# A spectral mixer and MLP on one core: batch 0's gathers on GpSimd's queue, the second stage two groups ahead, and a reordered opening

## The chip, the cores and the metric

The kernel runs on one core of one Trainium2 chip. The core has five engines, each with an instruction queue of its own that it works through in order: TensorE (PE; its weight loads are listed as PEld), VectorE (DVE), ScalarE (ACT), GpSimd (POOL) and SyncE (SP), which only issues transfers. Transfers (DMA) are issued from the queues of SP, ACT and POOL. The metric is the time of one execution on the device in microseconds (us). Each kernel is run several times, and the median is compared.

## The reference

The inputs are x of 8 x 3072 x 256, four parameters of a complex linear layer of width 256, and two weights of an MLP of width 2048; all is fp32.

```python
X = np.fft.rfft(x, axis=1)
Yr = Xr @ w_r - Xi @ w_i + b_r
Yi = Xr @ w_i + Xi @ w_r + b_i
Y = soft(Yr, 0.01) + 1j * soft(Yi, 0.01)     # sign(v) * max(|v| - 0.01, 0)
y = np.fft.irfft(Y, n=3072, axis=1)
h = y.reshape(8 * 3072, 256) @ w_in
out = (max(h, 0) + log1p(exp(-abs(h)))) @ w_out
```

## The kernel before, in words

The Fourier transform of 3072 = 96 x 32 points is split into small matrix products. For each batch:

- **s1** (first stage) is a product of length 96 over 512 columns of x; batch 0 has 16 of them, and their results stay on the chip in `a0`. For batch 1 ten such products are made ahead of the main loop, and the rest by `s1_four`, which does four matmuls of half width in one piece of the main loop; their results go to memory (`a_dr`).
- **s3** (second stage): `NP` = 12 groups. `load_a` gathers a group's operand `ap` from `a0` (for batch 0) in two halves, each from 4 rows to 128 rows of the chip's memory, into one of three buffers; four matmuls follow.
- **mix** (`mix_direct`): the complex layer. Its operand is split into a high part (ScalarE, rounded to fp32r) and a low part (VectorE, `less`, L119), and each product is three matmuls (`mm3`, L249 to L251), 24 a group. ScalarE also makes a negated copy (`minus`). Group 0 needs two corrected copies, called `real`. VectorE then adds the bias and does the soft threshold in three steps (L462 to L467; `z`, `cl`).
- **s4** (third stage): one matmul a group. Its result `d` goes partly to memory (`d_dr`) and, for batch 0, partly by two small gathers (`near`, L522) into `first_d`.
- **s5** (final stage): products over all groups give a block of tokens. For the first two blocks `first_tokens` turns four such products into the sums and differences B11, B21, T1 to T4 and B22, each split into a high and a low part.

The MLP is done with seven block products in place of eight, for two token blocks and two blocks of `w_in` at once (`ffn1`, banks `psc` and `pse`), a softplus, and `ffn2` into `pso`. The main loop has four slots for each step of it; `slot_products` and `slot_second` write them out. All spectral work of later batches, the splitting of the weights (`split_w`, eight of `w_in` and eight of `w_out`) and their stores are laid between the slots.

Everything stands in an order written out by hand. `first` lists the products ahead of the main loop and gives them negative indices up to -1; the main loop starts at index 0. `at(i, f)` puts anything else at an index, `turns` has for each weight the index of its split, that of its load and the staging buffer, and `later` holds work until the next index. At each index the program writes slot products, weight steps, the product, what `at` put there, and what was put off, and each engine gets its instructions in that order. A transfer that waits for its data holds up what stands behind it on its queue. Ahead of the main loop 6 banks of PSUM are used in turn (`psf`).

## Time and profile before

| | |
|---|---|
| median of 3 runs | 2607.09 us (2602.97 to 2609.22) |
| profiled execution, its own time | 2604.86 us |
| its span, first to last instruction | 2603.0 us |
| mean granted TensorE clock | 0.998 |
| PE busy | 2571.5 us (99% of the span) |
| ACT, DVE busy | 1672.2 us (64%), 1669.4 us (64%) |
| POOL busy | 166.8 us (6%) |

Busy times are sums over the whole span, and the opening (some 108 us ahead of the main loop) is a small part of it; stages have to be looked at one by one. A busy PE is not PE at its peak, since the ends of matmuls are modelled.

### The profile page before, as it was taken

The page shows a single profiled execution, that of the slowest core. Times are in us where ns is not written, and L with a number is a line of the kernel's source. Part 1 is how long each engine was busy: PE and PEld are TensorE (multiplying, and loading weights), DVE is VectorE, ACT ScalarE, POOL GpSimd, SP SyncE. Part 2 cuts the span into 40 slices and gives each one's busy share as a digit, 9 for nine tenths or more (in the row PEclk, how much of TensorE's full clock was granted, in tenths as well). Part 3 has the DMA queues.
Part 4 walks back from the last instruction along what each step waited for, and adds up shares of the span by engine and source line. Part 5 has one row for each costly group of instructions (what it writes and reads, how often), then busy time and mean ns, then how long its engine had stood idle before and what let it go on. Part 6 is the DMA issues. An engine that isn't in the chain of part 4 may idle for free.

```text
span 2603.0 us, 36237 instructions
## 1 busy us (share of the span) xinstructions
PE 2571.5 (99%) x13161; PEld 2128.4 (82%) x13161; DVE 1669.4 (64%) x2812; ACT 1672.2 (64%) x3025; POOL 166.8 (6%) x198
## 2 busy tenths in 40 slices
PE   7999999999999999999999999999999999999999
PEld 5677888888788888888888888888888888888887
DVE  4888775677566775666746767466674666645454
ACT  4676666666666666666666666666666666666665
POOL 2320000000000000000000000000000000000000
PEclk9999999999999999999999999999999999999999
DMA  8875555655646555565555665556645545445543
GB/s 248 255 237 189 176 185 167 214 185 160 206 159 195 169 181 190 166 193 186 163 191 178 187 194 163 184 174 182 210 159 169 180 158 188 140 159 183 175 150 113
DMA packets 187085, 472.53 MB, mean 182 GB/s; under 512 B 22252, under 2 KB 88844, under 8 KB 186908
## 3 DMA queue, kind: packets, MB, share of 16 engines
q1 hardware_dynamic: 182636, 466.01, 56.3%
q0 software_dynamic: 2912, 2.58, 0.4%
q8 instruction: 104, 1.70, 0.3%
q10 hardware_dynamic: 1360, 1.64, 0.2%
q14 instruction: 73, 0.60, 0.1%
HBM read 383.09 MB, written 82.71 MB: 179 GB/s over the span
## 4 chain that ended last, share of the span: by engine, by line
PE 94%; DVE 3%; DMA 1%; ACT 1%; issue 1%; POOL 0%; SPq 0%; DVEq 0%; POOLq 0%; ACTq 0%
PE pso L249 14%; PE pso L251 13%; PE pso L250 13%; PE psc L249 7%; PE psc L251 7%; PE psc L250 7%; PE pse L249 5%; PE pse L250 5%; PE pse L251 5%; PE psf L560 5%; PE psf L251 3%; PE psf L250 3%; PE psf L249 3%; PE psf L365 3%; PE psf L330 2%; PE psf L292 1%
## 5 line engine op out<-in xcount | busy, mean ns | idle before, releaser
L697 DVE TENSOR_TENSOR gl<-t,gh 128x512 fp32r<-128x512 f32 x768 | 532.1, 693 | 328.1 <-ACT gh L691 325.8
L676 ACT COPY t<-psc 128x512 f32<-128x512 f32 x576 | 337.8, 586 | 524.2 <-PE psc L251 522.0
L681 DVE TENSOR_TENSOR t<-pse,t 128x512 f32<-128x512 f32 x576 | 396.1, 688 | 401.0 <-ACT t L676 275.7
L249 PE MATMUL pso<-gh,w 128*128 128x512 f32 x1536 | 621.6, 405 | 0.0
L251 PE MATMUL pso<-gh,w 128*128 128x512 f32 x1536 | 600.1, 391 | 0.0
L250 PE MATMUL pso<-gl,w 128*128 128x512 f32 x1536 | 599.9, 391 | 0.0
L691 ACT CAST gh<-t 128x512 fp32r<-128x512 f32 x768 | 477.1, 621 | 60.9 <-PE pso L251 37.5
L687 ACT ACTIVATE t<-t 128x512 f32<-128x512 f32 x576 | 365.1, 634 | 65.9 <-DVE t L681 64.8
L249 PEld LDWEIGHTS pso<-gh,w 128*128 128x128 f32 x1536 | 289.8, 189 | 91.3 <-issue 41.9
L251 PEld LDWEIGHTS pso<-gh,w 128*128 128x128 f32 x1536 | 288.8, 188 | 62.6
L250 PEld LDWEIGHTS pso<-gl,w 128*128 128x128 f32 x1536 | 290.0, 189 | 49.3
L249 PE MATMUL psc<-y_sb,w 128*128 128x512 f32 x768 | 300.7, 392 | 3.0 <-ACT t L676 2.7
L251 PE MATMUL psc<-y_sb,w 128*128 128x512 f32 x768 | 299.8, 390 | 0.0
L250 PE MATMUL psc<-y_sb,w 128*128 128x512 f32 x768 | 298.8, 389 | 0.0
L599 POOL TENSOR_TENSOR y_sb<-raw,y_sb 128x512 fp32r<-128x512 f32 x69 | 104.7, 1518 | 2148.1 <-ACT y_sb L596 2148.1
L249 PE MATMUL pse<-y_sb,w 128*128 128x512 f32 x576 | 226.1, 393 | 3.1 <-DVE t L681 3.0
L250 PE MATMUL pse<-y_sb,w 128*128 128x512 f32 x576 | 224.4, 390 | 0.0
L251 PE MATMUL pse<-y_sb,w 128*128 128x512 f32 x576 | 224.4, 390 | 0.0
L249 PEld LDWEIGHTS psc<-y_sb,w 128*128 128x128 f32 x768 | 144.2, 188 | 36.0 <-ACT t L676 4.8
L251 PEld LDWEIGHTS psc<-y_sb,w 128*128 128x128 f32 x768 | 144.2, 188 | 31.2
L250 PEld LDWEIGHTS psc<-y_sb,w 128*128 128x128 f32 x768 | 144.2, 188 | 29.9
L498 DVE TENSOR_TENSOR shrunk<-z,cl 64x256 f32<-64x256 f32 x336 | 141.1, 420 | 6.2
(163 smaller groups left out, 3344.9 us busy)
## 6 DMA issues: line engine op xcount, KB each, us to landing
w<-w_dr SPq DMA_DIRECT2D x190, 896.0 KB
w<-w_dr SPq DMA_DIRECT2D x185, 512.0 KB
out_y<-ot SPq DMA_DIRECT2D x96, 256.0 KB
dp<-d_dr SPq DMA_DIRECT2D x57, 384.0 KB
ap<-a_dr SPq DMA_DIRECT2D x168, 128.0 KB
d_dr<-d SPq DMA_DIRECT2D x84, 256.0 KB
x<-in_x SPq DMA_DIRECT2D x104, 192.0 KB
a_dr<-a SPq DMA_DIRECT2D x102, 192.0 KB
```

Of the source, the lines that this page charges most:

```text
L249: nc.tensor.matmul(ps, wh, xh, start=start, stop=False, skip_group_check=more)
L250: nc.tensor.matmul(ps, wh, xl, start=False, stop=False, skip_group_check=more)
L251: nc.tensor.matmul(ps, wl, xh, start=False, stop=stop, skip_group_check=more)
L365: nc.tensor.matmul(xv[:, g, k], t[:, g, k * P:(k + 1) * P], g1_t[:, g].rearrange("p (c s) -> p c s", c=2), start=True, stop=True,)
L498: v.tensor_tensor(out=t[dst], in0=z[src], in1=cl[src], op=ALU.subtract)
L560: nc.tensor.matmul(ps[:, t - blk * BLK:t - blk * BLK + n], d_sb[b, blk // 2, n2 // 4][0][:, n2 % 4, k * P:(k + 1) * P], d_sb[b, blk // 2, ...
L599: eng.tensor_tensor(out=lo, in0=raw[j], in1=hi.bitcast(F32), op=ALU.subtract)
L676: nc.scalar.copy(t, banks[bank])
L681: nc.vector.tensor_tensor(out=t, in0=banks[bank], in1=t, op=ALU.add)
L687: nc.scalar.activation(t, banks[bank] if bank else t, AF.Softplus)
L691: nc.scalar.copy(gh, ct[key, what])
L697: nc.vector.tensor_tensor(out=gl, in0=ct.pop((key, what)), in1=gh.bitcast(F32), op=ALU.subtract)
```

## The change

It rewrites the order ahead of the main loop:

- Two matmuls on a tile of ones come first on PE.
- Gathers of batch 0 (`load_a`): four halves stay on SP's queue (the first of groups 0 to 3), twenty go to GpSimd's. Before, fifteen were on SP's and nine on GpSimd's. They may be asked for as soon as s3 of three groups before is done.
- s3 runs two groups ahead of the mix; every third group's operand has a buffer of its own (`l`), which the staging of two weights leaves.
- The constants `g1` come in five pieces rather than three, and most of them, the bias and the first weight behind the first gathers; the two mixing matrices come earlier and are split earlier.
- The copies `real` move from GpSimd to VectorE.
- The last group's second small gather is issued by SP (before: ACT).
- Twelve s1 products of batch 1 rather than ten stand ahead of the main loop, two of them between the last two s4; one `s1_four` less is in the main loop. Their stores are held until just ahead of the main loop.
- s5 is done in another order, and `first_tokens` is rewritten for it; one `snap` in the first step of the main loop stands earlier.

```diff
-        (1, 1, -48, -63, 'dp', 0),
+        (1, 1, -46, -51, 'dp', 0),
         (0, 0, -43, -49, 'raw', 1),
-        (1, 2, -38, -44, 'l', 0),
+        (1, 2, -38, -44, 'x1', 0),
...
-        (0, 2, -23, -29, 'l', 0),
+        (0, 2, -23, -29, 'x1', 0),
         (1, 4, -18, -24, 'dp', 0),
-        (1, 0, -13, -19, 'w64', 1),
+        (1, 0, -14, -19, 'w64', 1),
...
+        elif b and c >= 10:
+            xt = fours[1][:, (c - 10) * 512:(c - 9) * 512]
...
-        store(a_dr[b][:, 2 * c:2 * c + 2, :], a[16:].rearrange("p (n c) -> p n c", n=2), ("a", b))
+        dst, src = a_dr[b][:, 2 * c:2 * c + 2, :], a[16:].rearrange("p (n c) -> p n c", n=2)
+        if c < 4:
+            store(dst, src, ("a", b))
+        else:
+            held.append((dst, src, ("a", b)))
...
-                (nc.gpsimd if g and gp > 2 else nc.sync).dma_start(t[:, g, :], a0[16 + 2 * gp + g:16 + N1:NG])
+                (nc.gpsimd if g or gp > 3 else nc.sync).dma_start(t[:, g, :], a0[16 + 2 * gp + g:16 + N1:NG])
...
-            l = w1_tile()
+            l = sb.tile([P, 2 * 768], F32R, tag="l", name="l", bufs=1) if gp % 3 == 2 else w1_tile()
...
-                    nc.gpsimd.tensor_copy(r, t[:, 0:2, :P])
+                    nc.vector.tensor_copy(r, t[:, 0:2, :P])
                     for o in (0, 64):
-                        nc.gpsimd.memset(r[:, :, o:o + 1].bitcast(F32), 0.0)
+                        nc.vector.memset(r[:, :, o:o + 1].bitcast(F32), 0.0)
...
-                    (nc.scalar if gp >= 10 else nc.gpsimd).dma_start(first_d[2 * gp + g::NG].rearrange("q n c -> q (n c)"), dg[:4 * 12, g])
+                    (nc.gpsimd if gp < 10 else nc.sync if g and gp == NP - 1 else nc.scalar).dma_start(first_d[2 * gp + g::NG].rearrange("q n c -> q (n c)"), dg[:4 * 12, g])
...
         if what == 0:
             y_sb[key] = sb.tile([P, 16 * BLK], F32R, tag="y0", name="y_sb", bufs=1)
-            whole(key, B11, ps)
-            keep(key, 0, ps)
-        elif what == 1:
-            whole(key, B21, ps)
-            first_ps.append(ps)
+            both = sb.tile([P, 2 * BLK], F32, tag="raw", name="raw", bufs=1)
+            raw[0], raw[1] = both[:, :BLK], both[:, BLK:]
+            raw[2] = sb.tile([P, BLK], F32, tag="t", name="t", bufs=5)
+            a(tokens(key, B11)[0], ps)
+            a(raw[0], ps)
+            low(B11, raw[0])
         elif what == 2:
-            keep(key, 1, ps)
+            a(raw[1], ps)
             v(out=raw[0], in0=ps, in1=raw[0], op=ALU.subtract)
-        else:
-            raw[2] = sb.tile([P, BLK], F32, tag="t", name="t", bufs=5)
+            a(tokens(key, T1)[0], raw[0])
+        elif what == 3:
+            held_ps.append(ps)
             v(out=raw[2], in0=ps, in1=raw[0], op=ALU.subtract)
             v(out=raw[1], in0=ps, in1=raw[1], op=ALU.subtract)
-            split_token(key, T2, 2, nc.vector)
-            split_token(key, T3, 1, nc.vector)
+            a(tokens(key, T2)[0], raw[2])
+            a(tokens(key, B22)[0], ps)
+            low(T2, raw[2])
+        else:
+            a(tokens(key, B21)[0], ps)
+            a(tokens(key, T3)[0], raw[1])
+            low(B21, ps)
+            low(T3, raw[1])
+
+            low(T1, raw[0])
...
+        ones = sb.tile([P, 512], F32, tag="t", name="ones", bufs=5)
+        nc.vector.memset(ones, 1.0)
+        for _ in range(2):
+            nc.tensor.matmul(psf(), ones[:, :P], ones, start=True, stop=True)
         nc.gpsimd.dma_start(g3_sb, g3)
...
-        for i in range(NP + 3):
-            if i < NP:
-                first.append(("s3", 0, i))
-            if i >= 3:
-                first.append(("s4", 0, i - 3))
-            if 1 <= i <= NP:
-                first.append(("mix", 0, i - 1))
-
-        first += [("s1", 1, c) for c in range(4, 10)]
-        first += [("s5", j, k) for j, k in ((0, 0), (0, 1), (1, 0), (1, 1))]
+        first += [("s3", 0, 0), ("s3", 0, 1)]
+        for i in range(NP):
+            if i + 2 < NP:
+                first.append(("s3", 0, i + 2))
+            if i >= 2:
+                first.append(("s4", 0, i - 2))
+            first.append(("mix", 0, i))
+        first += [("s4", 0, NP - 2), ("s1", 1, 4), ("s1", 1, 5), ("s4", 0, NP - 1)]
+        first += [("s1", 1, c) for c in range(6, 12)]
+        first += [("s5", j, k) for j, k in ((0, 0), (1, 0), (1, 1), (0, 1))]
...
-                at(max(t - 7, t0 + 16), load_a, b, i)
+                at(max(t - 7, t0 + 16, first.index(("s3", 0, max(i - 3, 0))) + t0 if i > 2 else t0), load_a, b, i)
...
-        for t, i, j in ((t0 + 1, 0, 4), (t0 + 4, 4, 12), (t0 + 18, 12, NG)):
+        for t, i, j in ((t0 + 2, 0, 4), (t0 + 16, 4, 8), (t0 + 18, 8, 12), (t0 + 26, 12, 18), (t0 + 32, 18, NG)):
             at(t, nc.sync.dma_start, g1_0[:, i:j], g1[:, NG + i:NG + j])
-        at(t0 + 5, nc.sync.dma_start, bias0, bias_0)
+        at(t0 + 17, nc.sync.dma_start, bias0, bias_0)
...
-            at(t0 + 2, load_mix, k)
-            at(t0 + 17 + k, split_mix, k)
+            at(t0, load_mix, k)
+            at(t0 + 13 + k, split_mix, k)
...
+        for i in range(4):
+            at(i - 4, release, 2)
...
-        plan_s1(1, 4, 4, 5)
+        plan_s1(1, 4, 4, 6)
```

What the change moves on three queues, at the places that the text below speaks of. First GpSimd's queue at the start, before (`a_78` is `a0`; L219 to L221 are GpSimd's steps of a weight, L402 and L404 the copies `real`):

```order
L774 DMA x_96<-in_g 128x256
L349 DMA ap<-a_78 128x1x256
L219 ISA
L219 TENSOR_TENSOR y_79<-wt,wu 128x256
L220 TENSOR_TENSOR wt<-wt,wu 128x128
L221 TENSOR_TENSOR y_79<-wt,wu 128x128
L349 DMA ap<-a_78 128x1x256
L402 COPY real<-w_242 128x256
L404 MEMSET real 128x2 x2
```

The same queue after the change (L366 are the gathers, L223 a step of another weight, L539 the small gathers into `first_d`):

```order
L810 DMA x_96<-in_g 128x256
L366 DMA ap<-a_78 128x1x256 x8
L219 ISA
L219 TENSOR_TENSOR y_79<-wt,wu 128x256
L220 TENSOR_TENSOR wt<-wt,wu 128x128
L221 TENSOR_TENSOR y_79<-wt,wu 128x128
L366 DMA ap<-a_78 128x1x256 x2
L223 TENSOR_TENSOR w_225<-wt,wu 128x512
L539 DMA dp<-d 4x12x256 x2
L366 DMA ap<-a_78 128x1x256 x2
```

Eight gathers now stand in one row ahead of the first weight's steps, and later ones behind a weight's step. VectorE's queue from its first instruction on, before (the first weight, staged in `dpt`, has steps L197 to L203; L119 on `wml` splits a mixing matrix, on `w` it makes the mix operand's low part):

```order
L197 TENSOR_SCALAR wt<-dpt 128x512
L198 SCALAR_TENSOR_TENSOR wt<-dpt,wt 128x512
L119 TENSOR_TENSOR wml<-stage,wmh 128x2x256
L201 SCALAR_TENSOR_TENSOR wt<-wu,wt 128x512
L202 TENSOR_SCALAR wu<-wt 128x512
L203 TENSOR_TENSOR wu<-dpt,wu 128x512
L119 TENSOR_TENSOR wml<-stage,wmh 128x2x256
L119 TENSOR_TENSOR w_242<-psf,w_242 128x4x128
```

And after the change (L419 and L421 are the copies `real`):

```order
L807 MEMSET ones 128x512
L119 TENSOR_TENSOR wml<-stage,wmh 128x2x256 x2
L119 TENSOR_TENSOR w_233<-psf,w_233 128x4x128
L419 COPY real<-w_233 128x256
L421 MEMSET real 128x2 x2
L419 COPY real<-w_233 128x256
L421 MEMSET real 128x2 x2
L197 TENSOR_SCALAR wt<-dpt 128x512
L198 SCALAR_TENSOR_TENSOR wt<-dpt,wt 128x512
L119 TENSOR_TENSOR w_245<-psf,w_245 128x4x128
```

The first weight's five steps and the copies `real` now follow the first low part. SP's queue at the end of the third stage, as one piece of the difference (`w_dr` are stores of split weights, of which `w_dr_84` is the fifth of `w_in`; `dp<-d` is a small gather into `first_d`):

```order
 L237 DMA w_dr_90<-wp 128x1024
-L534 DMA dp<-in_hm 96x1152
+L283 DMA x_97<-in_x 96x512
 L237 DMA w_dr_84<-y_79 128x1792
-L104 DMA a_dr<-y_79 96x512
-L309 DMA x_97<-in_x 48x2x512 x2
+L539 DMA dp<-d 4x12x256
+L237 DMA w_dr_80<-w_978 128x1792
+L179 DMA y_79<-in_w_in 128x2x512
+L326 DMA x_96<-in_x 48x2x512 x2
 L104 DMA a_dr<-y_79 96x512 x2
```

The last group's second small gather now stands on SP behind the store of that weight.

## Rows read from the trace of the kernel before

**Rows 1.** The page: busy time of each engine, share of the span, instructions.

```profile
PE 2571.5 (99%) x13161; PEld 2128.4 (82%) x13161; DVE 1669.4 (64%) x2812; ACT 1672.2 (64%) x3025; POOL 166.8 (6%) x198
```

**Rows 2.** Busy time (and instructions) of each engine by stretch; granted clock, DMA share, GB/s.

```profile
26.00:97.00 71.00, 59.17 (x411) 50.84 (x411) 59.68 (x109) 34.37 (x71) 30.35 (x50) 0.99 0.79 239
...
300.00:2500.00 2200.00, 2199.66 (x11302) 1835.38 (x11301) 1399.72 (x2349) 1424.65 (x2577) 109.27 (x114) 1.00 0.56 177
```

**Rows 3.** PE in order of time: two mixes a group apart, final stage, main loop.

```profile
48.94 0.68 PE L249 MATMUL psf<-wmh,w 128*128 128x256 f32 x1
...
53.56 0.68 PE L249 MATMUL psf<-wmh,w 128*128 128x256 f32 x1
...
103.17 5.47 PE L560 MATMUL psf<-dp 96*128 96x96 f32 x48
...
108.45 0.48 PE L249 MATMUL psc<-y_sb,w 128*128 128x512 f32 x1
```

**Rows 4.** PE's waits from 26 to 97 us: total, times, longest.

```profile
PE psf L251 <- DVE w L119: 4.6, 4, 2.3
...
PE psf L365 <- DMA ap<-a: 3.2, 4, 1.6
...
PE psf L512 <- DVE z L467: 2.2, 1, 2.2
```

**Rows 5.** VectorE in order of time: first low part, last step of the last threshold.

```profile
28.77 0.69 DVE L119 TENSOR_TENSOR w<-psf,w 128x512 fp32r<-128x512 f32 x1 [0.87 <-ACT w L388]
...
94.55 0.69 DVE L467 TENSOR_TENSOR z<-z,cl 128x512 f32<-128x512 f32 x1
```

**Rows 6.** VectorE's busy time (and instructions) in two stretches; clock, DMA share, GB/s.

```profile
0.00:28.70 28.70, 4.13 (x7) 1.00 0.80 233
...
28.70:95.25 66.55, 56.21 (x103) 1.00 0.83 250
```

**Rows 7.** VectorE's waits from 28.7 to 95.3 us: total, times, longest.

```profile
DVE z L465 <- PE psf L251: 2.8, 1, 2.8
...
DVE w L119 <- ACT w L388: 2.1, 2, 1.2
...
DVE y L228 <- POOL y L221: 1.4, 1, 1.4
```

**Rows 8.** PE in order of time, first stage: start, length, engine, line, operation.

```profile
5.46 7.81 PE L292 MATMUL psf<-xt,x 96*128 96x512 f32 x12 [5.46 <-DMA xt<-in_x]
...
13.11 7.03 PE L292 MATMUL psf<-dp,x 96*128 96x512 f32 x16
...
19.98 1.88 PE L292 MATMUL psf<-x,x 96*128 96x512 f32 x4
```

**Rows 9.** The chain that ended last, by time: an early gather on SP.

```profile
23.30 3.77 DMA ap<-a
```

**Rows 10.** The line of the gathers (L349): GpSimd's issues, and until its gathers landed.

```profile
L349 POOL DMA_DIRECT2D ap<-a x9: 685/697/721, 28.5 to 73.3; - x9
...
DMA to landing us min/median/max: 6.1/7.5/8.9
```

**Rows 11.** Busy time by stretch as in group 2: three stretches with different DMA shares.

```profile
24.00:28.00 4.00, 2.68 (x12) 1.26 (x10) 3.01 (x5) 3.45 (x8) 0.00 (x0) 1.00 0.27 96
...
46.00:84.00 38.00, 36.05 (x264) 32.05 (x262) 34.35 (x63) 21.33 (x46) 20.36 (x30) 1.00 0.89 261
...
90.00:94.50 4.50, 3.16 (x22) 2.33 (x20) 4.36 (x10) 2.52 (x5) 2.86 (x6) 1.00 0.55 166
```

**Rows 12.** Small gathers by GpSimd's queue (L522): 46 to 84 us, then 89 to 94.

```profile
DMA to landing us min/median/max: 4.9/6.3/8.5
...
DMA to landing us min/median/max: 2.3/2.5/2.6
```

**Rows 13.** ScalarE's queue in order of time: the last group's small gathers.

```profile
97.81 1.63 ACTq L522 DMA_DIRECT2D dp<-d  x2
```

**Rows 14.** PE in order of time: four first-stage matmuls in the main loop.

```profile
121.46 1.09 PE L330 MATMUL psf<-x,f 48*64 48x512 f32 x8
```

More of the change, by code (lines that the diff above doesn't have):

```diff
@@ L172, in load_w @@
             st = sb.tile([P, 1024], F32, tag="raw", name="w64", bufs=1)
-        elif place == "l":
-            st = sb.tile([P, 2 * 768], F32R, tag="l", name="w64", bufs=1).bitcast(F32)[:, :1024]
+        elif place == "x1":
+            st = fours[1][:, :1024]
         elif place == "w64":
@@ L296, in s1, with release @@
             return
-        a = a1[:, c % 4] if c < 8 else g1_0[:16 + N1, 4 * (c - 8) + 16:4 * (c - 8) + 20].rearrange("p g n -> p (g n)")
-        nc.scalar.copy(a, ps[:16 + N1, :])
-        store(a_dr[b][:, 2 * c:2 * c + 2, :], a[16:].rearrange("p (n c) -> p n c", n=2), ("a", b))
+        if c < 8:
+            a = a1[:, c % 4]
+        elif c < 10:
+            a = g1_0[:16 + N1, 4 * (c - 8) + 16:4 * (c - 8) + 20].rearrange("p g n -> p (g n)")
+        else:
+            a = sb.tile([P, 512], F32, tag="a", name="a")[:16 + N1]
+        nc.scalar.copy(a, ps[:16 + N1, :])
+        dst, src = a_dr[b][:, 2 * c:2 * c + 2, :], a[16:].rearrange("p (n c) -> p n c", n=2)
[3 more added lines that the diff above has]
+            held.append((dst, src, ("a", b)))
+    held = deque()
+    def release(n):
+        for _ in range(n):
+            store(*held.popleft())
     def load_four(b, c):
@@ L604, in put_split, with low @@
         split_token(*args) if early else later.append(lambda: split_token(*args))
-    first_ps = []
+    held_ps = []
     def first_tokens(what, ps):
         key = 0, 0
-        v = nc.vector.tensor_tensor
+        v, a = nc.vector.tensor_tensor, nc.scalar.copy
+        def low(i, src):
+            hi, lo = tokens(key, i)
+            v(out=lo, in0=src, in1=hi.bitcast(F32), op=ALU.subtract)
         if what == 0:
             y_sb[key] = sb.tile([P, 16 * BLK], F32R, tag="y0", name="y_sb", bufs=1)
-            whole(key, B11, ps)
-            keep(key, 0, ps)
-        elif what == 1:
-            whole(key, B21, ps)
-            first_ps.append(ps)
+            both = sb.tile([P, 2 * BLK], F32, tag="raw", name="raw", bufs=1)
[4 more added lines that the diff above has]
+            low(B11, raw[0])
@@ L619, in first_tokens @@
         elif what == 2:
-            keep(key, 1, ps)
+            a(raw[1], ps)
             v(out=raw[0], in0=ps, in1=raw[0], op=ALU.subtract)
-        else:
-            raw[2] = sb.tile([P, BLK], F32, tag="t", name="t", bufs=5)
+            a(tokens(key, T1)[0], raw[0])
+        elif what == 3:
+            held_ps.append(ps)
             v(out=raw[2], in0=ps, in1=raw[0], op=ALU.subtract)
             v(out=raw[1], in0=ps, in1=raw[1], op=ALU.subtract)
-            split_token(key, T2, 2, nc.vector)
-            split_token(key, T3, 1, nc.vector)
-            def second():
-                split_token(key, T1, 0, nc.vector)
-                whole(key, B22, ps)
-                third()
-            def third():
-                v(out=raw[2], in0=first_ps[0], in1=raw[2], op=ALU.subtract)
-                later.append(lambda: split_token(key, T4, 2, nc.vector))
+            a(tokens(key, T2)[0], raw[2])
+            a(tokens(key, B22)[0], ps)
+            low(T2, raw[2])
+        else:
+            a(tokens(key, B21)[0], ps)
[3 more added lines that the diff above has]
+            low(T1, raw[0])
+            def second():
+                v(out=raw[2], in0=ps, in1=raw[2], op=ALU.subtract)
+                nc.gpsimd.tensor_copy(tokens(key, T4)[0], raw[2])
+                low(B22, held_ps[0])
+                later.append(lambda: low(T4, raw[2]))
@@ L740, in slot_products @@
             ffn1(key, "e", S3, T3)
+            if not prev:
+                snap(key, C21, "c")
             softplus(key, C11)
             high(key, C11)
-            snap(key, C21, "c")
+            if prev:
+                snap(key, C21, "c")
             low(key, C11)
@@ L792, in plan_s1 @@
                 at(t - 2 if b == 1 else t - 4, fold, b, c)
-                at(-8 if (b, c) == (1, 5) else t - 7, load_four, b, c)
+                at(t - 7, load_four, b, c)
         def plan_mix(b, start, step):
@@ L829, in tile_spectral_mixer_mlp @@
                 product(t, s1, b, i)
-                at(t0 + 23 + 3 * (i - 4) if b and i >= 4 else t0 - 1 + b, load_x, b, i)
+                at(i - 27 if b and i >= 10 else t0 + 23 + 3 * (i - 4) if b and i >= 4 else t0 - 1 + 2 * b, load_x, b, i)
             elif what == "s3":
                 product(t, s3, b, i)
-                at(max(t - 7, t0 + 16), load_a, b, i)
+                at(max(t - 7, t0 + 16, first.index(("s3", 0, max(i - 3, 0))) + t0 if i > 2 else t0), load_a, b, i)
             elif what == "mix":
@@ L856, in tile_spectral_mixer_mlp @@
         for i, (t, src) in enumerate(((g3h, g3_hi), (g3l, g3_lo))):
-            at(3 * i - 9, nc.gpsimd.dma_start, t, src)
-        at(-10, nc.gpsimd.memset, fours[1][32:64, :1024], 0.0)
-        at(-1, nc.gpsimd.memset, fours[0][32:64, :1024], 0.0)
+            at(3 * i + 8, nc.gpsimd.dma_start, t, src)
+        at(-3, nc.gpsimd.memset, fours[1][32:64, :1024], 0.0)
+        for i in range(4):
+            at(i - 4, release, 2)
+        at(-4, nc.gpsimd.memset, fours[0][32:64, :1024], 0.0)
         at(-1, early.clear)
```

## The prediction, made before the change was run

> **What bounds the kernel now.** I read the page's busy line first, then busy time by stretch, then PE's and VectorE's waits in the stretch that stands out, and last the rows at its two ends. The page says PE is busy 99% of the span [rows 1], and from 300 to 2500 us it is busy 2199.66 of 2200 us [rows 2]: there only fewer matmuls would help. The opening is different. From 26 to 97 us, twelve groups of batch 0 pass through the second stage (s3), the mix and the third stage (s4), and PE is busy 59.17 of 71 us [rows 2]. A group that waits for nothing takes 53.56 - 48.94 = 4.62 us [rows 3], twelve take 55.4 us, so about 15.6 us of the stage are waiting. PE's named waits there are VectorE's low parts of the mix operand (4.6 us), gathers (3.2) and the last soft threshold (2.2) [rows 4]; the rest is many short ones.
>
> VectorE is the other half of the stage. Its first low part starts at 28.77 and its last threshold ends at 94.55 + 0.69 = 95.24 [rows 5]. In these 66.5 us it works 56.2 and idles 10.3 [rows 6]: 2.8 until the first mix product, 2.1 for ScalarE's evacuations, 1.4 for GpSimd's part of the first weight [rows 7], and smaller pauses. PE needs 55.4 us and VectorE 56.2, yet the stage takes over 66, since each waits for the other. All that the change can reach is these 10 to 15 us, some 2.5 us at the start and a few around the start of the main loop.
>
> **The change part by part.** *Two matmuls on ones.* The first twelve matmul records (six products, two records each) take 5.46 to 13.11, 7.65 us; the next sixteen 13.11 to 19.98, 0.43 us each [rows 8]. At that pace twelve take 5.2 us, so 2.5 us are lost, as if about six records had run at half pace, TensorE's 1.2 GHz level, until some 5 us after its first matmul (read from the pace alone: the profile's clock holds no change before 10 us). The new matmuls are four records of that size, 3.4 us at half pace, in the time before the first x lands (5.46), when PE has nothing to do. If they start near 1.5 us (my estimate) and the pace again rises 5 us after the first, one or two slow records stay of six: 2.0 us saved, bounds 0 (the pause before 5.46 undoes it) and 2.5.
>
> *First gathers.* They may start 2.0 us earlier, near 20.5. On SP a gather landed 3.77 us after its issue [rows 9], and the last half of the first group came at 23.30 + 3.77 = 27.07. Now that half comes by GpSimd's queue, where gathers took 6.1 to 8.9 us [rows 10]. I take a value just over the lower end, 6.3, because little else moves then: DMA share 0.27 from 24 to 28 against 0.89 from 46 to 84 [rows 11]. So it lands near 26.8, and VectorE's first low part moves from 28.77 to 28.5 only. Bounds: 26 (GpSimd at the 2.5 us of small gathers at low DMA load [rows 12], so that SP's half, 20.5 + 3.8, decides) and 31 (8.9).
>
> *Second stage two groups ahead, and VectorE's order.* VectorE gets more to do between its first low part and its last threshold: the first weight's five steps, which stood ahead (seven instructions, 4.13 us before 28.7 [rows 6], less two splits of 0.69: 2.8), and the copies called real, taken over from GpSimd (0.7 for two of half width by the 0.69 of 512 columns [rows 5], 1.0 with four tiny fills). Six instructions now follow the last threshold, two of some 0.6 and four of a quarter width: -2.0. So 56.2 + 2.8 + 1.0 - 2.0 = 58.0 us. Of the idle 10.3 us, the three waits of [rows 7], 6.3 us, should go: with two more groups evacuated ahead there is always a low part or a weight step at hand. What stays is 4.0; new is about 1 at the start, where the second real copy needs ScalarE's negation, which stands behind the second group's evacuation; against that, fewer gathers and loads in front of the weights on SP's queue give back some 1.5. I take 3.5, bounds 2 and 8. The last threshold then ends at 28.5 + 58.0 + 3.5 = 90.0, **5.2 us earlier**. PE does not forbid it: twelve groups from about 31 end near 87.
>
> *GpSimd's queue.* It was busy 30.35 of 71 us [rows 2]; eleven more gathers at 0.70 [rows 10] make 38, so it does not fill up. But it works in order, and a gather may stand behind a weight step that waits for VectorE. Going through its order with these durations, group 7's gathers go out behind the second weight's step, near 47, and land near 55, 1.4 us after PE wants them; group 10's, behind the fourth weight's, are 2.4 us late. I cost this at nothing: VectorE, 58 us of work against PE's 55.4, has low parts and weight steps ready at both places. Without that cover it is 3.8 us.
>
> *The end of the stage.* Two first-stage products, 0.86 us each, now stand between the last two s4, which covers most of the 2.2 us wait, and there are eight such products in place of six. After the last threshold PE has s4 (one product, 0.86) and six products (5.2), so it is free for the final stage (s5) 6 us after it, against 103.17 - 95.24 = 7.9 [rows 3]. But s5 contracts over all groups, and the last group's second half is now gathered on SP, behind the store of the fifth weight. That store waits for VectorE's four sums, two first steps, three more steps and a split: 4.9 us by the prices above. The store is 0.92 MB, 3.5 us at 261 GB/s [rows 11], and the gather 2.5 us more at its best [rows 12]. If the gather overtakes the store it lands 8.4 us after the threshold, if it follows it 10; now both are issued at 97.81 on ScalarE's queue [rows 13] and cost no wait. I take 9.2: 1.3 us back. The main loop starts at 90.0 + 9.2 + 5.3 = 104.5 in place of 108.45: **-3.9 us**.
>
> *Tokens and main loop.* The first token products wait on ScalarE and VectorE; in the new order the last of four s5 products has two ScalarE steps behind it in front of the loop's own, where five stood. I give it 1.0 us (0 to 2). The loop loses one of its pieces with four first-stage matmuls, 1.09 us on PE [rows 14], and two VectorE sums of 0.69: 1.0 us. Other moved loads and fills lie beside these and I cost them at nothing; the covers are PE's own queue and VectorE's.
>
> **Sum:** -3.9 - 1.0 - 1.0 = -5.9 us. The profiled execution took 2604.86 us (2603.0 of span and 1.9 around it), so 2599.0; it lies 2.2 under the median of the three runs, 2607.09, from which the same sum gives 2601.2. I say 2600.0.
>
> **Two rules weighed.** From 24 to 28 us almost nothing but SP's gathers moves, at 96 GB/s with a DMA share of 0.27 [rows 11], about 4 of 16 engines. The Trainium skill, "DMA: Bandwidth & Descriptors", section "Why a DMA increments its semaphore by 16 and not by 1", says a copy whose slowest dimension is 4 on one side uses four engines, on the hardware queues always the lowest, on GpSimd's queue four that rotate. The trace agrees on four; no row shows which. By that rule GpSimd's first gathers run side by side, which would take about 1.5 us more off the start.
>
> While VectorE worked 34.35 of 38 us and the DMA share was 0.89, small gathers on GpSimd's queue landed in 4.9 to 8.5 us; while it worked 4.36 of 4.5 us at a share of 0.55, in 2.3 to 2.6 [rows 11, 12]. So it is DMA load that makes them late, not VectorE. The Trainium skill, "SBUF — State Buffer", in its box on the "DVE blocks DMA" trap, says that GpSimd cannot write descriptors while VectorE runs an operation on two ports, which speaks against this change; here the trace disagrees in size, and the time it would give is rival 2's.
>
> **The rivals.** *1. GpSimd's gathers stay at 7.5 to 8.9 us and the cover fails.* The first low part starts at 31 and the 3.8 us show: 2.5 + 3.8 us back of 5.9, 2605. For it: every gather on that queue took at least 6.1 [rows 10]; against it: the two ends of [rows 12]. *2. Slower: the loop through three buffers closes.* A buffer is free when s3 of three groups before is done; then GpSimd may be held by a weight step (up to 6 us), issues for 1.4, the gather takes 8.9, s3 0.9: 17.2 us for three groups, 5.7 each, against 66.5/12 = 5.5 now. It decides from 16.6 us a loop. Nine such groups and three at the start's pace, 51.6 + 14, from 31 end near 97; with s5 1.3 later and the loop's 2 us given back to a further half-clock stretch, 2608; at 6.5 a group 2615. Against it: the hold is that long at few groups. *3. VectorE and PE both run full.* Idle falls to 2, the first low part comes at 26 to 27, s5 is not late: 3.5 + 1.3 us more, 2594; with fewer waits in the loop's first 50 us, 2591.
>
> **How the numbers follow.** Forecast (2596.5 to 2603.5) 0.60, rival 1 0.15, rival 2 0.10, rival 3 0.15. The range 2593 to 2606 leaves out the far ends of rivals 2 and 3 and takes in the bounds above. 0.2% is 5.2 us, about what a measurement of this kernel can tell. Faster: rival 3 and two thirds of the forecast, 0.55. Same: the rest of the forecast and rival 1, 0.35. Slower: 0.10.
>
> **What would show it.** Right: first products at 0.43 us a record from the third on; VectorE's first low part near 28.5, its idle time to the last threshold 2 to 5 us and that threshold near 90; PE's waits for low parts of the mix operand almost gone; s5 waiting 2 to 4 us for first_d; the loop's first matmul near 104.5; no change from 300 us on. Wrong: gathers on GpSimd's queue landing after 8 us or more with PE and then VectorE waiting for them, a last threshold after 94, or a stretch at half clock in s5 or the loop's start that was not there.

## The result: 0.61% slower

The changed kernel takes 2622.3 us (median of six runs, 2619.4 to 2624.7) and the kernel before, beside it, 2606.3. The ratio is 1.0061, with a 95% interval of 1.0048 to 1.0074. The forecast was 2600.0 and its range 2593 to 2606, so the time moved 16 us the wrong way.

All of it is lost ahead of the main loop. From the timelines of VectorE and PE, in us:

| | before | changed |
|---|---|---|
| first low part of the mix operand begins | 28.8 | 29.4 |
| first soft threshold ends | 37.0 | 41.8 |
| last soft threshold ends | 95.2 | 106.6 |
| s5 begins | 103.2 | 117.0 |
| main loop begins | 108.4 | 126.8 |
| from there to the end of the span | 2494.6 | 2494.0 |

That is 11.3 us more to the last threshold, 2.5 from there to s5, 4.6 within s5, and 0.6 back in the loop; that last figure says nothing, since the same stretch takes 2491.8 to 2496.9 us in the profiles of the experiments. The changed kernel by stretch, in the columns of [rows 2]:

```profile
26.00:97.00 71.00, 56.54 (x355) 50.97 (x355) 49.09 (x92) 29.08 (x60) 30.64 (x45) 0.86 0.79 221
28.70:38.80 10.10, 7.82 (x35) 7.58 (x36) 4.40 (x13) 4.15 (x10) 3.70 (x5) 0.50 0.88 270
42.40:45.60 3.20, 3.20 (x17) 3.20 (x17) 1.04 (x3) 2.44 (x5) 1.37 (x2) 0.50 0.93 276
66.30:69.50 3.20, 3.20 (x11) 2.17 (x10) 1.82 (x3) 1.86 (x4) 0.65 (x1) 0.50 0.82 201
86.80:90.00 3.20, 3.20 (x16) 3.15 (x15) 0.18 (x1) 1.24 (x3) 0.00 (x0) 0.50 0.88 265
116.96:126.80 9.84, 9.84 (x48) 9.84 (x49) 3.36 (x5) 4.08 (x8) 0.00 (x0) 0.52 1.00 315
126.80:131.00 4.20, 4.20 (x11) 3.15 (x12) 3.08 (x5) 1.69 (x3) 0.00 (x0) 0.50 1.04 414
300.00:2500.00 2200.00, 2198.49 (x11302) 1834.36 (x11302) 1399.41 (x2351) 1420.12 (x2570) 105.34 (x111) 1.00 0.57 178
```

In the second stage VectorE's busy time falls (49.09 us from 26 to 97, against 59.68), because it comes later. Five stretches run at half clock (0.50, TensorE's 1.2 GHz), some 34 us in all; the last begins in s5, takes in nearly the whole of it and goes on in the loop to 131 us. The kernel before has one of 3.4 us ahead of its main loop, from 95.7 us on. From 300 us on next to nothing has changed. PE's named waits ahead of the loop:

```profile
PE psf L382 <- DMA ap<-a: 10.3, 4, 4.0
PE psf L382 <- issue: 3.4, 1, 3.4
PE psf L577 <- DMA w_dr<-y: 3.3, 1, 3.3
PE psf L382 <- DMA y<-in_g: 1.5, 1, 1.5
```

PE waits 10.3 us for gathers, three times as long as in [rows 4], while the waits for low parts are gone. Two of these waits, for the gathers of groups 7 and 10, stand right ahead of the third and fourth stretch at half clock:

```profile
65.12 1.45 PE L382 MATMUL psf<-y,ap 128*128 128x128 f32 x8 [4.04 <-DMA ap<-a]
...
85.36 0.71 PE L382 MATMUL psf<-y,ap 128*128 128x128 f32 x4 [3.17 <-DMA ap<-a]
```

What VectorE did from its first low part to its last threshold, first as busy time and then as waits:

```profile
29.30:106.65 77.35, 64.75 (x403) 57.29 (x404) 58.36 (x108) 33.22 (x68) 34.64 (x52) 0.87 0.81 230
```

```profile
DVE z L479 <- PE psf L251: 3.8, 1, 3.8
DVE wt L197 <- DMA x<-in_w_out: 3.5, 1, 3.5
DVE wt L197 <- DMA w<-in_w_in: 2.7, 1, 2.7
DVE real L419 <- ACT w L409: 2.4, 1, 2.4
DVE wt L197 <- DMA dpt<-in_w_in: 2.3, 1, 2.3
DVE wt L197 <- DMA dpt<-in_w_out: 1.5, 1, 1.5
```

Its work is 58.36 us; its idle time is 77.35 - 58.36 = 19.0. The four lines of L197 are waits for weights to land, 10.0 us together. The chain of waits names the transfers behind both engines, with the time from start to landing:

```profile
24.80 8.09 DMA y<-in_g
...
34.89 6.66 DMA ap<-a
...
55.77 11.85 DMA dpt<-in_w_out
...
73.66 11.65 DMA ap<-a
```

These are a piece of the constant `g1` for group 2, the gather of group 3, a weight of `w_out`, and the gather of group 10. The gather of group 7 was late on its queue (GpSimd's, in order of time):

```profile
43.49 1.37 POOL L366 DMA_DIRECT2D ap<-a  x2 [2.70 <-PE psf L382]
52.61 1.27 POOL L223 TENSOR_TENSOR w<-wt,wu 128x512 f32<-128x512 f32 x1 [7.75 <-DVE wu L203]
53.83 1.25 POOL L539 DMA_DIRECT2D dp<-d  x2
55.07 1.38 POOL L366 DMA_DIRECT2D ap<-a  x2
```

L223, a step of a weight, waited 7.75 us for VectorE, and the gathers behind it were issued at 55.07, of which group 7's gave PE its longest wait, 4.0 us. In these microseconds memory was nearly still (46.5 to 52.2 us), since SP's queue stood too, 9.5 us up to 52.28, for the first store of `d_dr`:

```profile
46.50:52.20 5.70, 5.70 (x47) 5.60 (x47) 4.71 (x11) 2.43 (x5) 0.00 (x0) 1.00 0.25 54
```

The last two numbers are DMA share and GB/s; at 66 and 87 us the share is 0.8 to 0.9, and the two transfers that the chain names last, issued at 55.77 and 73.66 us, take 11.85 and 11.65 us to land.

### The profile page after: what moved, and what is told of

It is laid out like the page before. It is cut to its first block, busy times and chain, and to the rows that moved or that the text cites. A ratio compares the mean times of both kernels' runs of the same rounds, so it can differ in the third digit from the quotient of the medians.

```text
span 2620.8 us, 36242 instructions
## 1 busy us (share of the span) xinstructions
PE 2583.6 (99%) x13161; PEld 2139.8 (82%) x13161; DVE 1670.0 (64%) x2817; ACT 1671.9 (64%) x3024; POOL 174.9 (7%) x204
## 4 chain that ended last, share of the span: by engine, by line
PE 92%; DVE 3%; DMA 2%; ACT 1%; issue 1%; POOL 0%; SPq 0%; DVEq 0%; ACTq 0%; POOLq 0%
PE pso L249 13%; PE pso L251 13%; PE pso L250 13%; PE psc L249 6%; PE psc L251 6%; PE psc L250 6%; PE pse L249 5%; PE psf L577 5%; PE pse L250 5%; PE pse L251 5%; PE psf L250 3%; PE psf L251 3%; PE psf L249 3%; PE psf L382 3%; PE psf L347 2%
## 5 line engine op out<-in xcount | busy, mean ns | idle before, releaser
L249 PE MATMUL pso<-gh,w 128*128 128x512 f32 x1536 | 620.5, 404 | 0.0
L249 PEld LDWEIGHTS pso<-gh,w 128*128 128x128 f32 x1536 | 289.3, 188 | 90.0 <-issue 40.6
L249 PE MATMUL psc<-y_sb,w 128*128 128x512 f32 x768 | 301.1, 392 | 1.2 <-ACT t L705 0.9
L249 PE MATMUL pse<-y_sb,w 128*128 128x512 f32 x576 | 226.5, 393 | 5.7 <-DVE t L710 5.6
L249 PEld LDWEIGHTS psc<-y_sb,w 128*128 128x128 f32 x768 | 144.4, 188 | 33.7 <-ACT t L705 2.7
L249 PE MATMUL psf<-wmh,l 128*128 128x256 f32 x536 | 154.3, 288 | 0.0
```

The lines of the kernel that those rows point to most:

```text
L249: nc.tensor.matmul(ps, wh, xh, start=start, stop=False, skip_group_check=more)
```

## The experiments

Every kernel was timed five to eleven times beside the kernel before. "Stage" is the time from the first threshold's end to the last one's, "to loop" from there to the main loop, both from one profile, so that 2 us there are no finding.

| | kernel | median us | ratio, 95% interval | first threshold | stage | to loop |
|---|---|---|---|---|---|---|
| | before | 2606.3 | | 37.0 | 58.3 | 13.2 |
| | changed | 2622.3 | 1.0048 to 1.0074 | 41.8 | 64.8 | 20.2 |
| e1 | changed, gathers as before | 2616.9 | 1.0026 to 1.0051 | 43.0 | 58.2 | 20.5 |
| e2 | changed, last small gather on ACT | 2623.7 | 1.0051 to 1.0078 | 41.0 | 67.7 | 20.0 |
| e3 | changed, no ones | 2624.9 | 1.0055 to 1.0080 | 42.6 | 68.0 | 20.3 |
| e4 | before, gathers on GpSimd | 2610.0 | 1.0007 to 1.0024 | 40.3 | 60.3 | 12.2 |
| e5 | changed, requests as before but one load | 2617.7 | 1.0025 to 1.0050 | 47.5 | 55.9 | 20.7 |
| e6 | e5, gathers as before | 2616.8 | 1.0024 to 1.0049 | 43.3 | 58.3 | 19.9 |
| e7 | changed, end as before | 2617.7 | 1.0030 to 1.0055 | 41.3 | 66.2 | 13.9 |
| e8 | changed, wait ahead of s5 filled | 2619.5 | 1.0033 to 1.0060 | 41.0 | 68.5 | 17.0 |
| e9 | changed, requests as before | 2615.4 | 1.0020 to 1.0043 | 41.0 | 58.2 | 20.7 |
| e10 | e9, end as before | 2612.2 | 1.0008 to 1.0027 | 39.1 | 63.2 | 13.2 |
| e11 | e10, gathers as before | 2609.3 | 0.9998 to 1.0016 | 41.9 | 57.6 | 13.2 |
| e12 | e11, one group ahead | 2603.4 | 0.9978 to 0.9996 | 35.6 | 58.8 | 13.2 |
| e13 | before, two groups ahead | 2609.8 | 1.0002 to 1.0019 | 40.8 | 59.8 | 12.4 |
| e14 | changed, one group ahead | 2616.2 | 1.0022 to 1.0045 | 37.8 | 62.8 | 20.2 |
| e15 | e12, gathers on GpSimd | 2607.4 | 0.9989 to 1.0007 | 37.2 | 62.0 | 13.2 |
| e16 | e12, `real` on GpSimd | 2604.0 | 0.9977 to 0.9995 | 36.5 | 56.2 | 13.2 |
| e17 | before, requests late | 2616.5 | 1.0028 to 1.0053 | 47.9 | 59.6 | 12.3 |
| e18 | e12, no ones | 2604.3 | 0.9983 to 1.0001 | 36.5 | 57.4 | 13.2 |

The theories: A, the gathers on GpSimd's queue; B, the late requests; C, the clock; D, the end of the stage; E, two groups ahead.

**Gathers (e1, e4, e15).** One line differs:

```diff
-                (nc.gpsimd if g or gp > 3 else nc.sync).dma_start(...)
+                (nc.gpsimd if g and gp > 2 else nc.sync).dma_start(...)
```

> The changed kernel (2622.3 us, 16.0 over the kernel before) with only the gathers split between the queues as before: 15 on SP, 9 on GpSimd. Theory A (the gathers on GpSimd's queue): there PE waits 10.3 us for gathers where it waited 3.2, and three of the half-clock stretches follow such a wait; then this gives 9 to 14 us back, 2608 to 2613, and PE's waits for ap fall to 3 to 4 us. Theory B (late requests): VectorE waits 10.0 us for weights and PE 1.5 us for a piece of the constant g1, because these are asked for later; then the gathers on SP push the weights back further, and the time stays at 2618 to 2626. Theory D (the end of the stage): the last small gather on SP and the half clock in the final stage cost 7 us of the 16; then the time falls by no more than 9, and the final stage still runs at half clock.

> The kernel before with one part of the change alone: all gathers of batch 0 but four on GpSimd's queue. Theory A: the second stage of one group ahead has no cover for late gathers, so this alone is 8 to 16 us slower: 2614 to 2622, with PE's waits for ap at 10 us or more in place of 3.2. Theory B: the gathers free SP's queue for the weights, so that this alone costs 0 to 5 us: 2606 to 2611.

> The fastest kernel so far (requests, end and lead as before; 2603.4 us) with the gathers on GpSimd's queue as in the change. Theory A: 2 to 5 us slower, as on the kernel before (2.8) and between the runs with the requests and the end as before (3.0): 2605.5 to 2608.5. If that loss came from two groups ahead, within 1.5 us: 2602 to 2605.

Undoing the move gives 5.4 us back, less than theory A said; alone it costs 2.8, where theory A had 8 to 16, and on e12 4.0. The stage is longer with the move in all three pairs, by 6.6 us (e1), 3.2 (e15) and 2.0 (e4, by itself no finding). In e1 PE's waits for gathers are halved, but the one for the piece of `g1` grows from 1.5 to 4.9 us:

```profile
PE psf L382 <- DMA ap<-a: 5.1, 5, 1.8
PE psf L382 <- DMA y<-in_g: 4.9, 1, 4.9
```

So A is a part of the loss, one of several.

**Requests (e5, e6, e9, e17).** e9's edit (e5 and e6 lack the load's -65, e17 is the reverse on the kernel before):

```diff
-        (1, 1, -46, -51, 'dp', 0),
+        (1, 1, -50, -65, 'dp', 0),
...
-        for t, i, j in ((t0 + 2, 0, 4), (t0 + 16, 4, 8), (t0 + 18, 8, 12), (t0 + 26, 12, 18), (t0 + 32, 18, NG)):
+        for t, i, j in ((t0 + 1, 0, 4), (t0 + 4, 4, 12), (t0 + 18, 12, NG)):
-        at(t0 + 17, nc.sync.dma_start, bias0, bias_0)
+        at(t0 + 5, nc.sync.dma_start, bias0, bias_0)
...
-            at(t0, load_mix, k)
-            at(t0 + 13 + k, split_mix, k)
+            at(t0 + 2, load_mix, k)
+            at(t0 + 17 + k, split_mix, k)
```

> The changed kernel with the loads of the opening asked for as before: the constants g1 in three pieces, the middle one (groups 4 to 11) and the bias ahead of the first gathers, the mixing matrices two steps later, the first weight four steps earlier. Theory B (late requests): in the run with the gathers as before PE stood 4.9 us for the second piece of g1 and the clock then fell to half for 10.24 us, some 5 us of work; both should go here, and VectorE's wait for the first weight too: 8 to 11 us back, 2611 to 2614. Theory A (GpSimd's gathers): the first three gathers on that queue landed at 27.7 to 30.6 us and hold the second stage whatever the constants do: 2618 to 2622.

> The kernel of the last run with the gathers split as before too. Left of the change are then the second stage two groups ahead, the end of the stage, the tokens, the ones. If A and B add up, 5.4 us (measured for the gathers alone) and 8 to 11 make 2606 to 2609, level with the kernel before; if the late constant was behind what the gathers seemed to cost, the two overlap and it is 2609 to 2613. If two groups ahead is itself a loss (rival E), it stays above 2613.

In e5 and e6 the third number of `turns`, the weight's step, was moved and its load, the fourth, was not. VectorE's waits in e5:

```profile
DVE wt L197 <- DMA dpt<-in_w_in: 34.5, 1, 34.5
```

The step stood ahead of the first low part, which came at 40.0 us, and still the kernel was 4.6 us faster than the changed one; the gathers as before on top of it (e6) bring 0.8. e9 moves the load too:

> The requests of the opening as before, this time with the load of the first weight too (asked for 14 steps earlier, its first step 4 steps earlier); in the run with the requests as before only the step had been moved and not the load, so that VectorE stood 34.5 us for it and its first low part came at 40.0 us. Theory B (late requests): that low part now comes at 29 to 31 us, PE's stand before it goes, and the last threshold ends 5 to 9 us sooner than 103.4 us: 2608 to 2613. Theory A (GpSimd's gathers): the first low part comes back to 30 us and the time does not follow, since the gathers of groups 7 and 10 hold PE: 2615 to 2619.

It gives 6.9 us back, to 2615.4, which by the number alone is what theory A had (2615 to 2619). The first threshold ends where it did (41.0); the stage is 6.6 us shorter. VectorE's waits ahead of the loop, and PE's for gathers:

```profile
DVE wt L197 <- DMA dpt<-in_w_in: 21.1, 1, 21.1
DVE z L479 <- PE psf L251: 5.5, 1, 5.5
```

```profile
PE psf L382 <- DMA ap<-a: 5.2, 3, 3.9
```

The one wait for a weight left is that for the first, ahead of all work. The gathers are still on GpSimd's queue, and group 7's is issued no sooner (at 56.10 us, behind a weight's step that waited 6.99 us). But PE's three waits are now for groups 2, 3 and 8, no longer for 7 and 10, which theory A had named; a gather on that queue takes at most 9.8 us to land in place of 12.5, and between 48 and 109 us nothing runs at half clock. So B does not act at the start, as expected, but later: through the weights' steps, and through gathers that land late while the late loads do. How much each of the two gives is not shown.

> The kernel before with one part of the change alone: the constants g1 in five pieces, the second and the bias behind the first gathers, the mixing matrices sooner, the first weight's load 14 steps later and its first step 3 later. Theory B: the second piece of g1 is wanted by the third group's second stage and comes 3 to 5 us late, and the clock falls behind it; one group ahead the third group is wanted 3.4 us later than two groups ahead, so that part of it is covered: 3 to 6 us slower, 2610 to 2613. If only two groups ahead makes the requests late, within 2 us: 2605 to 2609.

e17 costs 9.9 us, but not by what was expected: the weight's first step came ahead of the first low part, as in e5, and PE waited for it.

```profile
PE psf L251 <- DVE w L119: 11.1, 3, 8.4
```

It shows what a late load ahead of VectorE's urgent work costs, and does not isolate the constants.

**The end (e2, e7, e8).** e7 puts all eight s1 behind both s4 and the small gather on ACT; e2 has the small gather alone; e8 adds four products ahead of s5 (the second piece, its condition and its reshaping left out):

```diff
-        first += [("s4", 0, NP - 2), ("s1", 1, 4), ("s1", 1, 5), ("s4", 0, NP - 1)]
-        first += [("s1", 1, c) for c in range(6, 12)]
+        first += [("s4", 0, NP - 2), ("s4", 0, NP - 1)]
+        first += [("s1", 1, c) for c in range(4, 12)]
...
-                    (nc.gpsimd if gp < 10 else nc.sync if g and gp == NP - 1 else nc.scalar).dma_start(...)
+                    (nc.scalar if gp >= 10 else nc.gpsimd).dma_start(...)
```

```diff
+                    for _ in range(4):
+                        at(t - 1, lambda: nc.tensor.matmul(psf(), g1_0[:, 0], g1_0[:, 0:4], start=True, stop=True))
```

> The changed kernel with only the last small gather of first_d issued on ScalarE's queue again, as before, in place of SP's. Theory D: the final stage starts 2 to 3 us sooner after the last threshold (10.4 us now, 7.9 before), PE's idle time before it shrinks from 3.3 us to under 1.5, and the half-clock stretch of 13.65 us that begins with it shortens or goes: 2615 to 2619. Theories A and B: the loss lies before the last threshold (11.3 of 18.4 us at the loop's start), so this gives 1 to 3 us: 2619 to 2622.

> The changed kernel with the end of the second stage as before: no first-stage products between the last two s4, all eight behind them, and the last small gathers on ScalarE's queue. Theory D2: the last group's evacuation on ScalarE stood behind two first-stage evacuations and a weight's cast (s4 ended near 108.5, the evacuation began at 110.44, where the kernel before had 0.04 us between); without them the final stage starts 2 to 3 us sooner, its wait of 3.3 us goes, and the half-clock stretch shrinks: 2614 to 2618. If the final stage's clock falls whatever PE did before it, only the 1 to 2 us of the evacuation come back: 2620 to 2622.

> The changed kernel with four products on constants (eight records, about 3.4 us at full clock, their result unused) put on PE right ahead of the final stage, where it now stands 3.3 us. Theory C (an idle PE is charged twice, by the wait and by a fall to half clock after it): the final stage then takes 5.5 us in place of 10.0 and the loop starts at full clock; 4 to 7 us back, 2615 to 2618. If the clock falls for another reason, the final stage stays at 10 us and the time at 2621 to 2624.

e2 brings nothing: the queue of the small gather alone is not what is late. ScalarE in the changed kernel, in order of time (ACT its work, ACTq its transfers):

```profile
108.64 0.94 ACT L233 CAST y<-y 128x896 fp32r<-128x896 f32 x1 [2.08 <-DVE wt L198]
...
109.49 1.06 ACT L305 COPY y<-psf 112x512 f32<-112x512 f32 x2
110.44 0.60 ACT L534 COPY d<-psf 128x512 f32<-128x512 f32 x1
111.07 0.65 ACTq L539 DMA_DIRECT2D dp<-d  x1
```

s4 of the last group ends near 108.5; its evacuation (L534) begins at 110.44, behind a weight's cast, which waited 2.08 us, and two evacuations of s1 (L305). e7 takes these two away, though not the cast: L534 begins 2.9 us after the last threshold in place of 3.9, and with all eight s1 products behind it PE has work until s5, which begins 8.6 us after the threshold; it is 13.9 us to the loop in place of 20.2. There the two small gathers are issued 1.6 and 0.9 us ahead of the store of the fifth weight. In the changed kernel and in e2 s5 begins just as that store has landed (by the chains at 116.88 and 118.59 us), although in e2 both small gathers are issued, on ACT's queue, 1.0 and 0.3 us ahead of it. So the late evacuation brings the gathers up against the store; whether that or PE's lack of work weighs more is not shown. PE from s5 on in the changed kernel

```profile
116.96 10.03 PE L577 MATMUL psf<-dp 96*128 96x96 f32 x48 [3.29 <-DMA w_dr<-y]
126.80 0.77 PE L249 MATMUL psc<-y_sb,w 128*128 128x512 f32 x1
```

and in e8, from the added products on:

```profile
118.60 2.84 PE L877 MATMUL psf<-y 128*128 128x512 f32 x6 [1.54 <-ACT y L305]
121.28 5.44 PE L577 MATMUL psf<-dp 96*128 96x96 f32 x48
126.56 0.48 PE L249 MATMUL psc<-y_sb,w 128*128 128x512 f32 x1
```

The products (L877) still waited 1.54 us and s5 began later after the threshold, yet s5 took 5.44 us in place of 10.03 and the loop began 3.2 us sooner after the threshold. Theory C holds there: an idle PE is paid for twice (the whole time, 2619.5, lies between what was expected with C and without). All twenty profiles agree: in the eight in which PE stands 3.2 to 3.4 us ahead of s5, it is 9.8 to 10.2 us from its beginning to the loop; in the eleven with 0.6 us or less, and in e8, 5.3 to 5.4.

**The lead (e10 to e14).** One group ahead:

```diff
-        first += [("s3", 0, 0), ("s3", 0, 1)]
+        first += [("s3", 0, 0)]
         for i in range(NP):
-            if i + 2 < NP:
-                first.append(("s3", 0, i + 2))
+            if i + 1 < NP:
+                first.append(("s3", 0, i + 1))
```

> The same with the end of the second stage as before too (no first-stage products between the last two s4, last small gathers on ScalarE's queue). The end gave 4.6 us by itself; if it adds up with the requests, this is 4 to 5 us under the run with the requests alone, and the final stage runs at full clock in 5.5 us. If the late first_d is only replaced by another wait, under 2 us.

> The same with the gathers split as before too; left of the change are two groups ahead with its buffer, the copies called real on VectorE, the ones, the tokens and the loop's piece. Theory B: with requests, end and gathers back nothing is left that loses, and what is left gains: 2600 to 2606, at or under the kernel before. Rival E (two groups ahead loses by itself, since a gather is wanted one group sooner than its buffer and queue allow): 2608 to 2613.

> The kernel of the run before this one with the second stage one group ahead of the mix, as before. If two groups ahead gives VectorE the cover that the prediction counted on (4 of its 10.3 us of idle time), this is 2 to 5 us slower than that run; rival E: 2 to 5 us faster; if the gathers decide and not the lead, within 1.5 us.

> The kernel before with one part of the change alone: the second stage two groups ahead of the mix, with its extra buffer and the two weights staged elsewhere. Rival E: a second-stage product that waits for its gather stands on PE's queue ahead of a mix that is ready, so that PE idles at the third and fourth group (3 to 5 us, and a fall of the clock behind it): 2610 to 2616. The prediction's view (more cover for VectorE): 2601 to 2605.

> The changed kernel with the second stage one group ahead, nothing else undone. Rival E, if it adds up: 6 us back, 2614 to 2618. If late constants and gathers hold the stage whatever the lead, under 2 us: 2620 to 2623.

e10 and e11 come down by some 3 us each, about what these runs can tell. e12 is 5.9 us under e11, e14 6.1 under the changed kernel, and e13 2.5 over the kernel before: theory E, three times. The first threshold says where: it ends at 39 to 43 us in each kernel two groups ahead, at 35.6 to 40.3 in each one group ahead (but for e5 and e17). In the three pairs the lead makes it 6.3 (e11), 4.0 (changed) and 3.8 us (e13) later; of the 6.3, 2.2 stand already at the end of s1 in that profile. PE at the start of e11 (L382 is s3; the L249 rows stand for the mix):

```profile
29.29 2.46 PE L382 MATMUL psf<-y,ap 128*128 128x128 f32 x8 [0.74 <-ACT w L397]
...
34.87 0.56 PE L249 MATMUL psf<-wmh,w 128*128 128x256 f32 x1
...
39.49 0.28 PE L249 MATMUL psf<-wmh,w 128*128 128x256 f32 x1
...
43.17 2.05 PE L382 MATMUL psf<-y,ap 128*128 128x128 f32 x8 [3.17 <-DMA ap<-a]
```

and of e12:

```profile
28.52 1.22 PE L382 MATMUL psf<-y,ap 128*128 128x128 f32 x4 [0.46 <-DMA ap<-a]
29.40 0.56 PE L249 MATMUL psf<-wmh,w 128*128 128x256 f32 x1
...
33.50 1.06 PE L382 MATMUL psf<-y,ap 128*128 128x128 f32 x8
...
40.45 1.13 PE L382 MATMUL psf<-y,ap 128*128 128x128 f32 x8 [1.32 <-DMA ap<-a]
```

In e11 three groups' s3 stand ahead of the first mix (34.87); then group 3's s3 stands 3.17 us for its gather, and the next mix (44.88) waits behind it in PE's order. Its operand was there ten microseconds before, by VectorE in e11:

```profile
34.28 0.68 DVE L119 TENSOR_TENSOR w<-psf,w 128x512 fp32r<-128x512 f32 x1
```

In e12 the first mix begins at 29.40, two mixes are done ahead of group 3's s3, and that stands 1.32 us.

**What is left (e3, e16, e18).** These undo the change's lines on the ones or on `real`.

> The changed kernel without the two products on ones. Theory C (the clock): the early products let PE run at full clock from 7.99 on, but PE then stands from about 24 to 27 us, and the stretch at half clock from 28.64 to 38.88 is not theirs; without them the first stage ends 1.5 to 2.5 us later, and the time changes by less than 2 us: 2620 to 2625. If the early products bring the clock's fall forward into the second stage, the stretch of 10.24 us shortens and the time falls by 2 to 5: 2617 to 2620.

> The fastest kernel so far with the copies called real on GpSimd again. VectorE stood 2.5 us for the second of them there; the kernel before had PE stand 1.0 us for GpSimd's copy. If the copies on VectorE are a gain, this is 1 to 3 us slower, 2604.5 to 2606.5; if VectorE's wait costs, 1 to 2 us faster, 2601 to 2602.5.

> The fastest kernel so far (2603.4 us) without the two products on ones. The prediction gave them 2.0 us, and their removal cost 2.6 in the changed kernel: 2605 to 2606.5 here. If the gain in the first stage is given back later, within 1 us of 2603.4.

The ones are worth 2.6 us (e3) and 1.0 (e18), the copies' engine 0.6: both inside what the runs can tell. e12 and e16 beat the kernel before, by 0.13% and 0.14%, with intervals that leave out no change, but by less than the 0.2% named ahead.

## Why the prediction was wrong, point by point

- **The step that failed** is VectorE's idle time: "What stays is 4.0 ... I take 3.5, bounds 2 and 8", and with it the last threshold at 90.0. Its work was right (58.0 forecast, 58.36 measured), its idle time was 19.0. The ground given was that "there is always a low part or a weight step at hand". The lead puts an extra s3 ahead of the first mix and every waiting s3 ahead of a ready mix, and the weights' steps were not at hand, because their loads were late.
- **"Other moved loads and fills lie beside these and I cost them at nothing."** With the requests of this kind as before, e9 gains 6.9 us, as much as any other part undone. The cover named, the queues of PE and VectorE, was itself waiting for these loads.
- **GpSimd's queue.** Groups 7 and 10 were rightly named as late, by 1.4 and 2.4 us; PE waited 4.0 for the one and 3.2 for the other, which by the chain took 11.65 us to land. Landing was taken from [rows 10]; now it is

```profile
DMA to landing us min/median/max: 5.4/8.1/12.5
```

  The cover failed, as rival 1 had it. Its price of 3.8 us is near the 2.8 to 5.4 of e4, e15 and e1; that is partly luck, since in e9 PE waits for neither of the two groups, though the gathers stay on that queue.
- **The first low part**: 28.5 forecast, 29.4 measured. That step held, within its bounds.
- **The end**: s5 9.2 us after the threshold; it was 10.4. The store was in the sum, the evacuation's place on ScalarE behind a cast and two others was not (e2, e7). That s5 itself would run at half clock (10.03 us for 5.47) stands in no term, only among the signs of being wrong.
- **The clock** was counted in the first products alone. In the sum, a wait of PE had its own length as price; here all five stands of 2 us or more between the first stage and the loop were followed by a stretch at half clock, and one of the two (2.3 and 2.2 us) in the kernel before. The Trainium skill, "TensorE: Matmul & The Clock Gate", section "HAM oscillation — how this bites in real kernels", says that waits for transfers between bursts of matmuls let the clock fall again and again. The trace agrees: five stretches, each behind a stand of PE.
- **Tokens and loop**: 2.0 us forecast, 0.6 measured, and by the scatter of that time neither is shown. **Ones**: 2.0 forecast, 2.6 and 1.0 measured.
- **Sums.** By the prices beside them the gather would land 7.4 us after the threshold if it overtakes the store and 10.9 if it follows it, where 8.4 and 10 are given; the 9.2 taken is the middle of either pair. Rival 1's 2605 starts from 2599.0; from the 2600.0 that was said it would be 2606.3.
- **Rival 2** had the sign and, at 2608 to 2615, most of the size; GpSimd held by a weight's step is in it (7.75 us, 6 expected), and so is its loop: from the start of s3 of group 4 to that of group 7 18.1 us passed, and from there to the second half of group 10's 20.2, against 17.2. The waits for weights and the lead are not in it. It was given 0.10; each late thing had been priced by itself.

The parts undone one at a time from the changed kernel give 5.4, 6.9, 4.6 and 6.1 us, 23 together, where all four undone together (e12) give 18.9: they overlap by some 4. Reckoned against the kernel before that was timed beside each, it is 26 and 20, an overlap of 6. Left open is how e9's 6.9 us divide between constants, bias, mixing matrices and the first weight, and how much of the gathers' loss is the queue's order and how much memory traffic.

## What to carry to other kernels

Issuing a product further ahead on an in-order engine helps only if its operand is there: otherwise it holds up the product that is ready. Before a transfer is moved to make room, look for who waits for it now and later; a load that costs nothing today may do so only because it is early. A wait of PE should be priced with the half clock behind it, and an evacuation by its place in ScalarE's order.

## What had not been expected of the hardware

While GpSimd's first three gathers ran, SP's almost stopped. The changed kernel by queue from 24.5 to 26.5 us (packets, bytes, share of 16 engines; q0 is GpSimd's, q1 SP's):

```profile
q0 software_dynamic: 103, 0.28, 61.0%
q1 hardware_dynamic: 12, 0.01, 3.0%
```

and the kernel before in the same stretch:

```profile
q1 hardware_dynamic: 192, 0.19, 27.1%
```

GpSimd's three did run side by side, on about ten engines' worth (61% of 16), as had been weighed ahead; but SP's three gathers, of groups 0 to 2, whose data s3 needs as well, hardly moved meanwhile, and VectorE's first low part came at 29.4 us where it had come at 28.8. The Trainium skill, "DMA: Bandwidth & Descriptors", section "Queues, rings and completion order", says that an engine takes turns between its queues packet by packet; 12 packets against 103 do not look like turns, though no run here shows whether SP's were ready.
